# A new order of the seven products of a pair, and whole transposes with ScalarE copies in the late attention bursts

## The chip, the core and the metric

The kernel runs as one program on one core of a Trainium2 chip. The metric is the device time of one execution in microseconds (us); lower is better. A core has a matrix engine (TensorE, "PE" in the profile; its weight loads are listed apart as "PEld"), a vector engine (VectorE, "DVE"), a scalar engine (ScalarE, "ACT"), a general engine (GpSimd, "POOL") and an engine that here only issues DMAs (SyncE, "SP"). Each engine runs its own instructions in the order in which the program holds them, and waits on semaphores for the others.

## The reference

Chunked attention, and on its result a feed-forward layer with softplus, all in float32:

```python
# q, k, v: (8, 8, 576, 64); chunks of 64 positions
scores = scale * np.matmul(q_c, k_c.transpose(0, 1, 2, 4, 3))
scores = scores - np.max(scores, axis=-1, keepdims=True)
attn = np.exp(scores)
attn = attn / (np.sum(attn, axis=-1, keepdims=True) + 1e-09)
out = np.matmul(attn, v_c)
# x = out as (4608, 512); w_in (512, 2048), w_out (2048, 512)
h = x @ w_in
g = np.maximum(h, 0.0) + np.log1p(np.exp(-np.abs(h)))
return g @ w_out
```

## The kernel before

**The work.** A float32 operand is split into a high and a low part, and a product becomes three matmuls (high by high, low by high, high by low). The 4608 rows of x are nine blocks of 512; `w_in` is cut into 16 column chunks of 128, and `w_out` into 16 row chunks. For the first three blocks each chunk is one group of 12 matmuls for `x @ w_in` (L644) and one group of 12 for `g @ w_out` (L1004, called G2).

**The pairs.** The six later blocks are taken two at a time, in three *supers* (0, 1 and 2). In a super, two blocks and two chunks of `w_in` make a 2 by 2 product of block matrices, which is done with seven products of half the size in place of eight. This is a *pair*; a super has eight (named 0_0 to 0_7, and so on). `product(w, k)` issues product k: six matmuls (L788). The seven go into four PSUM banks, `BANK = (0, 1, 2, 3, 1, 2, 0)`: products 4, 5 and 6 add to the banks 1, 2 and 0. The banks lie in two PSUM tiles of two banks each, taken from a pool `pa` of two: one tile has the banks 0 and 3, the other the banks 1 and 2.

Around them stand small operations on 128 by 512 elements:
- the holds s0, s1 and s2 (`hold`, ScalarE, L794) copy bank 0, 1 and 2 to SBUF before the bank is added to;
- the mixes (`mix`, L807): d and c22 on GpSimd, e, f, f2 and c11 on VectorE. e reads bank 3, f reads bank 1, f2 bank 2, c11 bank 0; d needs s1 and s2, c22 needs d and e;
- four softplus operations (`soft`, ScalarE, L818, in super 2 L816): 10 reads bank 1, 01 reads bank 2, 11 reads the result of c22, and 00 that of c11.

The weights of a pair come from DRAM by two DMAs that GpSimd issues (`ring_load`, L745): part 0 (1024 KB) for products 0 to 3, part 1 (768 KB) for products 4 to 6. Each part has one buffer in supers 0 and 1, which is free when product 3, or product 6, is done.

**The order on PE.** In supers 0 and 1 a pair is the seven products, then two G2 groups of the pair before it; the second half of each super is G2 groups alone, for which the softplus results come back from DRAM (`spill_load`) and are split by ScalarE (`sp_hi`, L656) and VectorE (`sp_lo`, L660). In super 2 the second layer is done by seven products too (`sum_product`, L940, groups R): a pair is followed by two groups of six matmuls for the pair before, R1 and R0, and after the eight pairs come the groups R2 to R6.

**The attention bursts.** The attention of the later tiles of 128 rows runs beside this. A *burst* is two steps on PE (L608 and L520), each of which takes one `pa` tile: attention times values for two tiles, and the scores of the next two. Bursts stand after the pairs 2, 5 and 7 of supers 0 and 1 and once in each of their second halves. Between two bursts VectorE subtracts the maximum (L565, L570), ScalarE takes the exponential (L583), VectorE normalizes (L588 to L595) and turns the result. `blk_e4` does that with four transposes of 32 by 256 elements in each of two steps, Tf and Te (L544), so eight for a tile.

**What sets the order.** Nothing is ordered by hand but the list `seq` of PE's groups. `Plan` holds all tasks with an engine, a cost, what they need and an urgency, and plays them through ahead of time: a free engine takes the ready task with the lowest `urg`, and a task of `urg` 0 or more is held back when an urgent one is known to be ready within 0.5 us. The program's instructions are written in the order of the start times of this play. `take` names the pool slots that a task needs, and who frees them. The waits themselves aren't in the plan: the framework adds them from what each instruction reads and writes.

Of the kernel before, what the change touches and what calls it, by code (L numbers as in the profile page):

```python
# [160 lines left out]
def chunked_attention_softplus_ffn(  # L161
# [9 lines left out]
    nc = tc.nc  # L171
# [213 lines left out]
    def po_tile(n):  # L385
        return ps_o.tile([P, DM], F32, name=f"po{n}")
# [150 lines left out]
    def blk_e4(i, a):  # L537
# [126 lines left out]
    )  # L664
    X_SUMS = {0: ALU.add, 2: ALU.subtract, 3: ALU.add, 4: ALU.subtract, 6: ALU.add}
    BANK = (0, 1, 2, 3, 1, 2, 0)
    NX = 4
    PLACE = (1, 2, 0, 3, 6, 4, 5)

# [105 lines left out]
        eng.tensor_tensor(lo, x_of_product(n, k), hi.bitcast(F32), op=ALU.subtract)  # L775

    def product(w, k):
        if "bank" not in w:
            if w["in_po"]:
                w["bank"] = [po_tile(n) for n in range(4)]  # L780
            else:
                a, b = pa_tile(), pa_tile()
                w["bank"] = [a[:, 0], b[:, 0], b[:, 1], a[:, 1]]
        wts = w_image(w, k).rearrange("p (q k f) -> p q k f", q=2, k=2)
        hi, lo = (t.rearrange("p (k c) -> p k c", k=2) for t in x_image(k))
        for c in range(2):
            for n, (q, x) in enumerate(((0, hi), (1, hi), (0, lo))):
                nc.tensor.matmul(  # L788
                    w["bank"][BANK[k]], wts[:, q, c, :], x[:, c, :], start=k < NX and c + n == 0, stop=c == 1 and n == 2,
                    skip_group_check=True,  # L790
                )
# [3 lines left out]

    def mix(w, what):
        s1, s2, s3, f = (tmp_of(n) for n in range(4))
        x, y, z, v = w["bank"]
        out, a, b, op = {
            "d": (s2, s3, s2, ALU.subtract),  # L800
            "e": (s1, s1, v, ALU.add),
            "c22": (s1, s1, s2, ALU.add),
            "f": (f, y, s2, ALU.add),
            "f2": (f, f, z, ALU.subtract),
            "c11": (f, f, x, ALU.add),
        }[what]
        (nc.gpsimd if what in MIX_POOL else nc.vector).tensor_tensor(out, a, b, op=op)  # L807
# [92 lines left out]
    GI = 4  # L900

    def slot_of(k, j):
        return k + 4 * (j == FC // 2 - 2) if k < 2 else (FC // 2 * k + j + 2) % GI

    def g_image(k, j):
        if ("gi", k, j) not in live:
# [335 lines left out]
    for n in range(len(SUPERS)):  # L1242
        mine = pairs[n * FC // 2 : (n + 1) * FC // 2]
        for w in mine:
            seq += [f"P{k}_{w['name']}" for k in range(7)]
            seq += [f"G2_{v_['name']}" for v_ in behind[:1]]
            add_burst(n, 0, w["j"])
            seq += [f"G2_{v_['name']}" for v_ in behind[1:]]
            if n in BOTH and R_LAG <= w["j"] < FC // 2 - 1:
                seq += [f"R{k}_{w['j'] - R_LAG}" for k in (1, 0)]  # L1250
            behind = [] if n in BOTH else w["first"][::-1]
        if n in BOTH:
            NJ = FC // 2
# [40 lines left out]
    for key, (pv, ps) in bursts.items():  # L1294
# [40 lines left out]
        for n in range(2):  # L1335
# [11 lines left out]
            plan.add(f"norm{i}", "POOL" if pool else "DVE", 1.05 if pool else 0.65, partial(att_norm, i),  # L1347
                     [f"den{i}"], urg=d)
            gone = [f"V{FIRST_BLK - 1}"] if ps == F else [f"B{at}_{n}"]
            if i in SWAP_DVE:  # L1350
                plan.add(f"Tf{i}", "DVE", 1.76, partial(blk_e4, i, 0), [f"norm{i}"] + gone, urg=d)
                plan.add(f"Te{i}", "DVE", 1.76, partial(blk_e4, i, 1), [f"Tf{i}"], urg=d)
                swapped[i] = f"Te{i}"
            else:
                plan.add(f"Te{i}", "DVE", 0.65, partial(blk_e, i), [f"norm{i}"], urg=d)
                plan.add(f"swap{i}", "ACT" if i in SWAP_ACT else "SP", 4.8, partial(blk_swap, i), [f"Te{i}"] + gone, urg=d - SW_URG, kb=190, parts=8)
                swapped[i] = f"swap{i}"
# [55 lines left out]
    for at, w in enumerate(pairs):  # L1413
# [12 lines left out]
                     after=[f"ring{part}_{pairs[at - 1]['name']}"] if at else [])  # L1426
        for k in range(7):
            needs = [f"ring{k // NX}_{name}", f"xH{n}_{k}", f"xL{n}_{k}"]
            needs += [before[f"P{k}_{name}"]] + {4: [f"s1_{name}", f"s2_{name}"], 6: [f"s0_{name}", f"e_{name}"]}.get(k, [])
            take = []  # L1430
            if k == 0:
                rel = [[f"c11_{name}"], [f"soft10_{name}"], [f"soft01_{name}", f"f2_{name}"], [f"e_{name}"]]
                take = [("pa", rel[0] + rel[3]), ("pa", rel[1] + rel[2])]
                if w["in_po"]:
                    take = [(f"po{b}", rel[b]) for b in range(4)]
            plan.add(f"P{k}_{name}", "PE", PM, partial(product, w, k), needs, urg=1e6, take=take)
        for q in range(3):
            past = [f"soft00_{pairs[at - 1]['name']}", f"soft11_{pairs[at - 1]['name']}"] if at and not q else []
            plan.add(f"s{q}_{name}", "ACT", 0.59, partial(hold, w, q), [f"P{max(q, 2 * (q > 0))}_{name}"] + past, urg=-3 if n in BOTH else -2)
        for what, needs in (  # L1440
            ("d", ["s1", "s2"]), ("e", ["s0", "P3"]), ("c22", ["e", "d"]), ("f", ["d", "P5"]), ("f2", ["f", "P5"]),
            ("c11", ["f2", "P6"]),
        ):
            pool = what in MIX_POOL
            plan.add(f"{what}_{name}", "POOL" if pool else "DVE", 1.3 if pool else 0.69, partial(mix, w, what),
                     [f"{t}_{name}" for t in needs], urg=-2)
        a, b = (v_["name"] for v_ in w["first"])
        for i, jj, what in ((1, 0, "P5"), (0, 1, "P5"), (1, 1, "c22"), (0, 0, "c11")):
            kept = [f"lo{v_['name']}" for v_ in w["second"]] if j == FC // 2 - 1 else [f"us{name}"]
# [225 lines left out]
```

## Time and profile before

| what | value |
|---|---|
| runs shown | 829.07, 829.46 and 833.96 us, median 829.46 |
| the profiled execution | 831.35 us, its span in the profile 829.6 us |
| PE | busy 809.9 us, 98% of the span |
| PEld, DVE, ACT, POOL | 80%, 70%, 49%, 49% |
| granted TensorE clock | 0.995 |

The span goes from the first instruction to the last; the 1.75 us between it and the execution's own time lie outside of it. A busy time counts an engine from the start to the end of its instructions. Matmuls overlap: one of 512 columns is listed with 0.39 us, while the next starts 0.227 us after it. So the cost of a wait on PE is best read from the starts. A group of 12 that waits for nothing takes 2.72 us from its start to the start of the next, a product of six 1.36 us.

In the rows below, a row of the timeline has the start, the time, the engine, the source line, the operation and its operands, the count of instructions merged, and in brackets the idle time of the engine just before, with what ended it. A row of the waits has the engine and line that waited, what it waited for, the sum in us, how many times, and the longest. A row of the chain has start, time, engine and line, and the count.

### The profile page before, as it was taken

How to read it: one execution, taken by the hardware profiler on the slowest of the kernel's cores; microseconds unless marked ns; L12 is line 12 of the kernel's file. 1: busy time of each engine (PE TensorE's matmuls, PEld its weight loads, DVE VectorE, ACT ScalarE, POOL GpSimd, SP SyncE). 2: the span in 40 equal slices, each digit the busy share in tenths (PEclk: the TensorE clock that was granted, in tenths of full speed). 3: DMA queues.
4: the chain of work that ended last, by engine and by line, in shares of the span. 5: the costliest groups of instructions: out<-in, count | busy, mean ns of one | idle time of the engine just before them, and what ended most of it. 6: DMA issues, size and time to landing. Idle time of an engine off the chain costs nothing.

```text
span 829.6 us, 15582 instructions
## 1 busy us (share of the span) xinstructions
PE 809.9 (98%) x5675; PEld 661.9 (80%) x5675; DVE 581.2 (70%) x938; ACT 403.2 (49%) x664; POOL 404.3 (49%) x467
## 2 busy tenths in 40 slices
PE   8799999999999999999999999999999999999997
PEld 7687878888887888787888878888887788788786
DVE  4898997086478777657477878483789954575984
ACT  3767765345344574253434444443553644454551
POOL 1557559879975822221234212122177629982213
PEclk9899999999999999999999999999999999999999
DMA  9976758644674454777739527857647664566463
GB/s 218 239 187 190 207 164 244 188 112 127 149 198 113 111 146 158 219 187 213 197 127 257 158 64 242 227 153 213 203 130 258 209 228 167 202 234 231 150 206 68
DMA packets 202877, 151.27 MB, mean 182 GB/s; under 512 B 161136, under 2 KB 176752, under 8 KB 198576
## 3 DMA queue, kind: packets, MB, share of 16 engines
q1 hardware_dynamic: 189424, 99.66, 43.9%
q0 software_dynamic: 11232, 50.34, 18.9%
q8 instruction: 45, 0.74, 0.4%
q10 hardware_dynamic: 2144, 0.26, 0.2%
q14 instruction: 32, 0.26, 0.1%
HBM read 106.95 MB, written 41.94 MB: 179 GB/s over the span
## 4 chain that ended last, share of the span: by engine, by line
PE 77%; DVE 8%; DMA 4%; ACT 4%; POOL 3%; issue 3%; SPq 1%; DVEq 0%; POOLq 0%; ACTq 0%
PE po L1004 28%; PE pa L788 22%; PE pa L644 13%; PE po L940 9%; DVE g_lo L660 2%; PE pa L608 2%; DMA xb<-scratch 2%; PE pa L520 1%; DVE wib L807 1%; DMA images<-wib 1%; DVE ends L306 1%; POOL raw L875 1%; DVE eT L544 1%; DMA raw<-in_moe_w_in_dram 1%; POOL raw L865 1%
## 5 line engine op out<-in xcount | busy, mean ns | idle before, releaser
L807 POOL TENSOR_TENSOR wib<-wib 128x512 f32<-128x512 f32 x48 | 63.0, 1312 | 207.9 <-ACT wib L794 198.5
L1004 PE MATMUL po<-late,g_hi 128*128 128x512 f32 x420 | 128.8, 392 | 0.1
L544 DVE STREAM_TRANSPOSE eT<-qe 32x256 f32<-32x256 f32 x216 | 93.9, 435 | 3.0
L788 PE MATMUL pa<-wi_hi,xb 128*128 128x512 f32 x304 | 93.9, 390 | 0.4 <-DMA xb<-scratch 0.4
L1004 PEld LDWEIGHTS po<-late,g_hi 128*128 128x128 f32 x420 | 78.2, 188 | 16.9 <-DVE raw L1011 0.4
L788 PE MATMUL pa<-wib,xb 128*128 128x512 f32 x360 | 87.2, 395 | 0.7 <-DVE wib L775 0.7
L1004 PE MATMUL po<-wo_hi,g_lo 128*128 128x512 f32 x224 | 84.4, 393 | 0.8 <-DVE g_lo L660 0.7
L1004 PE MATMUL po<-wo_hi,g_hi 128*128 128x512 f32 x224 | 85.1, 396 | 0.0
L1004 PE MATMUL po<-wo_lo,g_hi 128*128 128x512 f32 x224 | 84.2, 392 | 0.0
L1004 PE MATMUL po<-late,g_lo 128*128 128x512 f32 x224 | 83.5, 390 | 0.3 <-DVE g_lo L660 0.3
L788 PEld LDWEIGHTS pa<-wib,xb 128*128 128x128 f32 x360 | 65.9, 188 | 18.7 <-ACT wib L794 4.5
L807 DVE TENSOR_TENSOR wib<-wib,pa 128x512 f32<-128x512 f32 x72 | 49.3, 685 | 42.4 <-PE pa L788 26.8
L660 DVE TENSOR_TENSOR g_lo<-ends,g_hi 128x512 fp32r<-128x512 f32 x64 | 53.3, 832 | 29.3 <-ACT g_hi L656 29.0
L652 ACT ACTIVATE u<-pa 128x512 f32<-128x512 f32 (+1 forms) x50 | 29.0, 579 | 92.2 <-PE pa L644 87.8
L794 ACT COPY wib<-pa 128x512 f32<-128x512 f32 x72 | 39.8, 587 | 56.9 <-PE pa L788 56.9
L656 ACT CAST g_hi<-ends 128x512 fp32r<-128x512 f32 x64 | 39.5, 617 | 57.6 <-PE po L1004 53.2
L788 PEld LDWEIGHTS pa<-wi_hi,xb 128*128 128x128 f32 x304 | 56.8, 188 | 13.1 <-issue 1.4
L788 PE MATMUL pa<-wi_lo,xb 128*128 128x512 f32 x152 | 59.2, 389 | 0.0
L660 DVE TENSOR_TENSOR g_lo<-u,g_hi 128x512 fp32r<-128x512 f32 (+1 forms) x32 | 31.1, 971 | 31.8 <-ACT g_hi L656 24.9
L1004 PEld LDWEIGHTS po<-wo_hi,g_lo 128*128 128x128 f32 x224 | 42.3, 189 | 10.9 <-DVE g_lo L660 2.1
L1004 PEld LDWEIGHTS po<-late,g_lo 128*128 128x128 f32 x224 | 42.0, 188 | 9.6 <-DVE g_lo L660 0.9
L1004 PEld LDWEIGHTS po<-wo_lo,g_hi 128*128 128x128 f32 x224 | 42.3, 189 | 8.7
(288 smaller groups left out, 1777.7 us busy)
## 6 DMA issues: line engine op xcount, KB each, us to landing
xb<-scratch POOLq DMA_DIRECT2D x19, 1024.0 KB, 6.0
xb<-scratch POOLq DMA_DIRECT2D x20, 768.0 KB, 7.1
raw<-in_moe_w_in_dram SPq DMA_DIRECT2D x16, 512.0 KB, 5.3
raw<-in_moe_w_out_dram SPq DMA_DIRECT2D x16, 512.0 KB, 5.0
scratch<-ends SPq DMA_DIRECT2D x16, 512.0 KB, 3.0
out_dram<-raw SPq DMA_DIRECT2D x28, 256.0 KB, 3.4
spill<-ends SPq DMA_DIRECT2D x14, 512.0 KB, 5.1
ends<-spill SPq DMA_DIRECT2D x14, 512.0 KB, 4.1
```

The costliest lines, as they stand in the source:

```text
L306: nc.vector.tensor_tensor(low, low, live.pop(("top", u)), op=ALU.add)
L544: nc.vector.transpose(live["eT", i][d : d + BL, tb], e[s : s + BL, kb])
L608: nc.tensor.matmul(pa[o, a, col : col + C], vt[r, 4 * j + 2 * h2 + c2, :], eT[r, :, 4 * c2 + 2 * j + h2, :], start=True, stop=True,)
L644: nc.tensor.matmul(ph, wt[:, c, :], x[:, ts_, c, :], start=(n == 0), stop=(n == 3 * KC - 1))
L652: nc.scalar.activation(w["u"], w["ph"], AF.Softplus)
L656: nc.scalar.copy(w["hi"], w["u"])
L660: (nc.gpsimd if pool else nc.vector).tensor_tensor(w["lo"], w["u"], w["hi"].bitcast(F32), op=ALU.subtract)
L788: nc.tensor.matmul(w["bank"][BANK[k]], wts[:, q, c, :], x[:, c, :], start=k < NX and c + n == 0, stop=c == 1 and n == 2, skip_group_check= ...
L794: nc.scalar.copy(tmp_of(n), w["bank"][n])
L807: (nc.gpsimd if what in MIX_POOL else nc.vector).tensor_tensor(out, a, b, op=op)
L940: nc.tensor.matmul(live["acc", ACC[k]][ct][:, cols], (w[:, q] if k > 1 else w[q])[:, ct * P : (ct + 1) * P], g[:, cols], start=k < 3 and j ...
L1004: nc.tensor.matmul(pos[w["m"]][t], terms[n][0][:, j * P : (j + 1) * P], terms[n][1], start=(w["first"] and n == 0), stop=n == 2 and (w["la ...
```

## The change

- In every pair the products run in the order 1, 2, 0, 3, 4, 5, 6. The two PSUM tiles are no longer taken together at the first product: that of the banks 1 and 2 is taken at product 1, that of the banks 0 and 3 at product 0.
- In a pair without a burst, one of the two G2 groups (in super 2: R1) moves from behind product 6 to between products 3 and 4. In a pair with a burst it stays between product 6 and the burst.
- The plan's needs follow: each hold needs its own product alone; product 4 needs s1, product 5 needs s2; a hold waits for the last readers of its own place of the pair before.
- For the tiles from 22 on (14 tiles) `blk_e2` transposes the whole 128 by 512 tile twice in place of the eight quarters, once into each of two buffers, and `blk_cross` has ScalarE copy four blocks of 32 by 256 from the one into the other. The burst's second step then needs these copies.

```diff
+    def blk_e2(i, a):
+        e = live["e", i].rearrange("p a j (u k) -> p u (a j) k", u=2)
+        if a == 0:
+            nc.vector.transpose(live["eA", i], e)
+            return
+        live["eT", i] = blk_et(i)
+        nc.vector.transpose(live["eT", i], e)
+        live.pop(("e", i))
+
+    def blk_cross(i):
+        ea, eT = live.pop(("eA", i)), live["eT", i]
+        for a in range(2):
+            for kb in range(2):
+                d, s = (2 * a + kb) * BL, (2 * a + 1 - kb) * BL
+                nc.scalar.copy(eT[d : d + BL, 1 - kb], ea[s : s + BL, kb])
...
+    ORDER = (1, 2, 0, 3, 4, 5, 6)
...
     def product(w, k):
-        if "bank" not in w:
-            if w["in_po"]:
-                w["bank"] = [po_tile(n) for n in range(4)]
-            else:
-                a, b = pa_tile(), pa_tile()
-                w["bank"] = [a[:, 0], b[:, 0], b[:, 1], a[:, 1]]
+        if k in (ORDER[0], ORDER[2]):
+            t = pa_tile()
+            w.setdefault("bank", {}).update({1: t[:, 0], 2: t[:, 1]} if k == 1 else {0: t[:, 0], 3: t[:, 1]})
...
     def slot_of(k, j):
-        return k + 4 * (j == FC // 2 - 2) if k < 2 else (FC // 2 * k + j + 2) % GI
+        return k + 4 * (j == FC // 2 - 1) if k < 2 else (FC // 2 * k + j + 2) % GI
...
+    CROSS = tuple(range(22, NPT))
...
-            seq += [f"P{k}_{w['name']}" for k in range(7)]
-            seq += [f"G2_{v_['name']}" for v_ in behind[:1]]
-            add_burst(n, 0, w["j"])
-            seq += [f"G2_{v_['name']}" for v_ in behind[1:]]
-            if n in BOTH and R_LAG <= w["j"] < FC // 2 - 1:
-                seq += [f"R{k}_{w['j'] - R_LAG}" for k in (1, 0)]
+            j = w["j"]
+            mid, end = (behind[:1], behind[1:]) if len(behind) > 1 else ([], behind)
+            mid, end = ([f"G2_{v_['name']}" for v_ in vs] for vs in (mid, end))
+            if n in BOTH and j >= R_LAG:
+                mid, end = [f"R1_{j - R_LAG}"], [f"R0_{j - R_LAG}"]
+                if j == FC // 2 - 1:
+                    mid, end = [], mid + end
+            burst_here = (n, 0, j) in bursts
+            seq += [f"P{k}_{w['name']}" for k in ORDER[:4]] + ([] if burst_here else mid)
+            seq += [f"P{k}_{w['name']}" for k in ORDER[4:]] + (mid if burst_here else [])
+            add_burst(n, 0, j)
+            seq += end
...
+            if i in CROSS:
+                plan.add(f"Tf{i}", "DVE", 0.69, partial(blk_e2, i, 0), [f"norm{i}"] + gone, urg=d)
+                plan.add(f"Te{i}", "DVE", 0.69, partial(blk_e2, i, 1), [f"Tf{i}"], urg=d)
+                plan.add(f"Tc{i}", "ACT", 1.6, partial(blk_cross, i), [f"Te{i}"], urg=d)
+                swapped[i] = f"Tc{i}"
...
-            needs += [before[f"P{k}_{name}"]] + {4: [f"s1_{name}", f"s2_{name}"], 6: [f"s0_{name}", f"e_{name}"]}.get(k, [])
+            needs += [before[f"P{k}_{name}"]] + {4: [f"s1_{name}"], 5: [f"s2_{name}"], 6: [f"s0_{name}", f"e_{name}"]}.get(k, [])
             take = []
-            if k == 0:
-                rel = [[f"c11_{name}"], [f"soft10_{name}"], [f"soft01_{name}", f"f2_{name}"], [f"e_{name}"]]
-                take = [("pa", rel[0] + rel[3]), ("pa", rel[1] + rel[2])]
+            if k == ORDER[0]:
+                take = [("pa", [f"soft10_{name}", f"soft01_{name}", f"f2_{name}"])]
+            elif k == ORDER[2]:
+                take = [("pa", [f"c11_{name}", f"e_{name}"])]
...
-            plan.add(f"s{q}_{name}", "ACT", 0.59, partial(hold, w, q), [f"P{max(q, 2 * (q > 0))}_{name}"] + past, urg=-3 if n in BOTH else -2)
+            plan.add(f"s{q}_{name}", "ACT", 0.59, partial(hold, w, q), [f"P{q}_{name}"] + past, urg=-3 if n in BOTH else -2)
```

More of the change, by code (lines that the diff above doesn't have):

```diff
@@ L797, in mix @@
         s1, s2, s3, f = (tmp_of(n) for n in range(4))
-        x, y, z, v = w["bank"]
+        x, y, z, v = (w["bank"][n] for n in range(4))
         out, a, b, op = {
@@ L1253, in chunked_attention_softplus_ffn @@
             NJ = FC // 2
-            seq += [f"R{k}_{j}" for j in range(NJ - R_LAG - 1, NJ) for k in (1, 0)]
+            seq += [f"R{k}_{j}" for j in range(NJ - R_LAG, NJ) for k in (1, 0)]
             seq += [f"R{k}_{j}" for k in range(2, 6) for j in range(NJ if k < 5 else NJ - SPREAD)]
@@ L1349, in chunked_attention_softplus_ffn @@
             gone = [f"V{FIRST_BLK - 1}"] if ps == F else [f"B{at}_{n}"]
-            if i in SWAP_DVE:
+            if i in CROSS:
[3 more added lines that the diff above has]
+                swapped[i] = f"Tc{i}"
+            elif i in SWAP_DVE:
                 plan.add(f"Tf{i}", "DVE", 1.76, partial(blk_e4, i, 0), [f"norm{i}"] + gone, urg=d)
@@ L1428, in chunked_attention_softplus_ffn @@
             needs = [f"ring{k // NX}_{name}", f"xH{n}_{k}", f"xL{n}_{k}"]
-            needs += [before[f"P{k}_{name}"]] + {4: [f"s1_{name}", f"s2_{name}"], 6: [f"s0_{name}", f"e_{name}"]}.get(k, [])
+            needs += [before[f"P{k}_{name}"]] + {4: [f"s1_{name}"], 5: [f"s2_{name}"], 6: [f"s0_{name}", f"e_{name}"]}.get(k, [])
             take = []
-            if k == 0:
-                rel = [[f"c11_{name}"], [f"soft10_{name}"], [f"soft01_{name}", f"f2_{name}"], [f"e_{name}"]]
-                take = [("pa", rel[0] + rel[3]), ("pa", rel[1] + rel[2])]
-                if w["in_po"]:
-                    take = [(f"po{b}", rel[b]) for b in range(4)]
+            if k == ORDER[0]:
+                take = [("pa", [f"soft10_{name}", f"soft01_{name}", f"f2_{name}"])]
+            elif k == ORDER[2]:
+                take = [("pa", [f"c11_{name}", f"e_{name}"])]
             plan.add(f"P{k}_{name}", "PE", PM, partial(product, w, k), needs, urg=1e6, take=take)
         for q in range(3):
-            past = [f"soft00_{pairs[at - 1]['name']}", f"soft11_{pairs[at - 1]['name']}"] if at and not q else []
-            plan.add(f"s{q}_{name}", "ACT", 0.59, partial(hold, w, q), [f"P{max(q, 2 * (q > 0))}_{name}"] + past, urg=-3 if n in BOTH else -2)
+            past = [f"{t}_{pairs[at - 1]['name']}" for t in (("soft11",), ("c22", "f"), ("d",))[q]] if at else []
+            plan.add(f"s{q}_{name}", "ACT", 0.59, partial(hold, w, q), [f"P{q}_{name}"] + past, urg=-3 if n in BOTH else -2)
         for what, needs in (
@@ L1444, in chunked_attention_softplus_ffn @@
             pool = what in MIX_POOL
+            past = [f"soft00_{pairs[at - 1]['name']}"] if at and what == "f" else []
             plan.add(f"{what}_{name}", "POOL" if pool else "DVE", 1.3 if pool else 0.69, partial(mix, w, what),
-                     [f"{t}_{name}" for t in needs], urg=-2)
+                     [f"{t}_{name}" for t in needs] + past, urg=-2)
         a, b = (v_["name"] for v_ in w["first"])
```

## The prediction

> **What bounds the kernel now.** I read the page's head first, then who PE and its weight loads wait for from 317 us on, where the pairs begin.
>
> ```profile
> span 829.6 us, 15582 instructions
> PE 809.9 (98%) x5675; PEld 661.9 (80%) x5675; DVE 581.2 (70%) x938; ACT 403.2 (49%) x664; POOL 404.3 (49%) x467
> ...
> 317.00:487.00 170.00, 169.61 (x1215) 138.56 (x1214) 116.72 (x206) 74.48 (x119) 45.10 (x59) 1.00 0.67 189
> ...
> PE pa L788 <- DMA xb<-scratch: 0.4, 2, 0.2
> ...
> PEld pa L788 <- ACT wib L794: 6.2, 24, 0.9
> PEld po L1004 <- DVE g_lo L660: 3.0, 5, 1.1
> ...
> PEld pa L788 <- DVE wib L775: 1.1, 1, 1.1
> ```
>
> PE is the bound: its matmuls fill 98% of the span, and from 317 to 487 us all but 0.39 of 170 us. The change adds and removes no matmul, and nothing before the first pair moves. So it can only gain what PE waits, and lose what it makes PE wait. The head hides the small waits; the weight loads show them. One number stands out: 24 waits for a hold (L794), and there are 24 pairs.
>
> ```profile
> 729.67 9.62 PE pa L788 x42
> 739.29 2.72 PE po L940 x12
> ...
> 366.61 1.07 ACT L794 COPY wib<-pa 128x512 f32<-128x512 f32 x2 [0.69 <-PE pa L788]
> 367.74 1.23 PEld L788 LDWEIGHTS pa<-wib,xb 128*128 128x128 f32 x6 [0.23 <-ACT wib L794]
> ...
> 371.95 0.39 PE L1004 MATMUL po<-wo_hi,g_hi 128*128 128x512 f32 x1
> ...
> 710.22 1.66 PE L788 MATMUL pa<-wib,xa 128*128 128x512 f32 x6 [0.52 <-ACT wib L794]
> ```
>
> Twelve matmuls in 2.72 us make 0.227 each, so a pair's 42 should take 9.52; the chain gives 9.62. The missing 0.10 lies at product 4: s1 and s2, both after product 2, end at 367.68, and the weights of product 4 come at 367.74, 0.06 behind. Product 4 writes bank 1 and s2 reads bank 2, so the wait is for the whole two-bank tile.
>
> **The change part by part.** First what PE gets back. Listed idle understates a loss: a matmul is listed with 0.39 but its successor starts after 0.227, so 0.16 is to be added, and about 0.10 for the restart (the same 0.10 as above).
>
> *Holds.* With the order 1, 2, 0, 3 both holds are done two products or more before product 4. 23 ordinary waits at 0.10 are 2.3 us; the long one, in pair 2_3 (0.52 + 0.16 + 0.10), is 0.8. If holds are late on ScalarE, products 0 and 3 (2.72 us), and in most pairs a group besides, cover them.
>
> *Ring loads and the first pair of super 1.*
>
> ```profile
> 382.83 1.30 POOL L807 TENSOR_TENSOR wib<-wib 128x512 f32<-128x512 f32 x1 [9.88 <-ACT wib L794]
> 385.01 1.30 POOL L807 TENSOR_TENSOR wib<-wib 128x512 f32<-128x512 f32 x1 [0.89 <-DVE wib L807]
> 386.25 0.57 POOL L745 DMA_DIRECT2D xb<-scratch  x1
> ...
> xb<-scratch POOLq DMA_DIRECT2D x20, 768.0 KB, 7.1
> ...
> 392.83 0.70 PE L788 MATMUL pa<-wi_hi,xb 128*128 128x512 f32 x2 [0.21 <-DMA xb<-scratch]
> ...
> 497.96 1.19 PE L788 MATMUL pa<-wib,xb 128*128 128x512 f32 x4 [0.69 <-DVE wib L775]
> ```
>
> Counted back from the wait at 392.83 (two groups, 5.44, and products 4 to 6, 4.18), product 3 is done at about 383. But part 0 of the next weights is issued at 386.25, behind d and c22 on GpSimd's queue. Now d starts when products 1 and 2 are held, so it is over before product 3 ends, and the load can go some 3 us sooner; PE's way from product 3 to the next pair stays the same length. Two waits of 0.2 + 0.16 + 0.10 go: 0.9 us. Part 1 has less room before a burst pair (one group less, 8.2 us from product 6 to product 4), but lands in 7.1 even now, while part 0 is under way beside it; I price it at 0. The wait at 497.96 is product 6 for its x image; a G2 group now stands between, so 0.69 + 0.16 + 0.10 = 0.95 goes.
>
> *The transposes.*
>
> ```profile
> L544 DVE STREAM_TRANSPOSE eT<-qe 32x256 f32<-32x256 f32 x216 | 93.9, 435 | 3.0
> L532 DVE STREAM_TRANSPOSE ka<-qe x5: 698/705/711, 70.8 to 283.6; 128x512 f32<-128x512 f32 x5
> L656 ACT CAST g_hi<-ends 128x512 fp32r<-128x512 f32 x64 | 39.5, 617 | 57.6 <-PE po L1004 53.2
> L660 DVE TENSOR_TENSOR g_lo<-ends,g_hi 128x512 fp32r<-128x512 f32 x64 | 53.3, 832 | 29.3 <-ACT g_hi L656 29.0
> ...
> 653.37 1.01 ACT L879 CAST wib<-wib 128x256 fp32r<-128x256 f32 x3
> ...
> 630.57 1.80 DVE L544 STREAM_TRANSPOSE eT<-qe 32x256 f32<-32x256 f32 x4
> 633.53 1.23 DVE L660 TENSOR_TENSOR g_lo<-ends,g_hi 128x512 fp32r<-128x512 f32 x1
> 634.81 0.50 PE L1004 MATMUL po<-wo_hi,g_lo 128*128 128x512 f32 x1 [0.68 <-DVE g_lo L660]
> ```
>
> Eight quarters at 0.435 are 3.48 us a tile; two whole ones (nearest row: the same operation at L532, 0.705) are 1.41. VectorE gets back 2.07 on each of 14 tiles, 29 us. ScalarE gets four copies a tile; no row has 32 by 256, the nearest is 128 by 256, three in 1.01, so 1.3 us for four, at most 1.6, some 20 in all on an engine that is 49% busy. On PE this is worth only what stood behind transposes: the five waits for g_lo. Their 3.0 us of idle weight loads, less 0.13 each by the measure above (0.23 of idle cost 0.10), are 2.35 on PE. The longest is at 634.81, behind a row of four quarters and the next tile's work; I take three of the five, 1.4 us, between bounds of 0 and 2.35. Against it: a set of copies can stand before a g_hi on ScalarE. A group lasts 2.72, and hi (0.62) and lo (0.83) with their hand-overs need some 1.6, so 1.6 us of copies costs at most 0.5, in the four tiles whose copies fall in second halves: 2.0 at worst, taken as 0.
>
> One rule of the Trainium skill speaks against this 1.4: "SBUF — State Buffer", section "Who interferes with whom", has a VectorE instruction with two SBUF inputs shut out while GpSimd reads SBUF. That would leave g_lo slow (1.23 here) whatever the transposes take, and the sum at 0 to 0.7 for this term.
>
> Together: 2.3 + 0.8 + 0.9 + 0.95 + 1.4 = 6.35 us.
>
> *What the new order makes PE wait for.* Product 1 now opens a pair, and takes the PSUM tile of banks 1 and 2, which the pair before gives back after softplus 10 and 01, f and f2. Before, product 0 opened with the other tile.
>
> ```profile
> 370.84 1.28 ACT L818 ACT_TABLE_LOAD   x1 [3.15 <-PE pa L788]
> 372.83 0.69 DVE L807 TENSOR_TENSOR wib<-pa,wib 128x512 f32<-128x512 f32 x1 [2.42 <-ACT ends L818]
> 374.28 0.60 ACT L818 ACTIVATE ends<-pa 128x512 f32<-128x512 f32 x1 [1.55 <-DVE wib L807]
> ...
> 726.33 0.69 DVE L807 TENSOR_TENSOR wib<-pa,wib 128x512 f32<-128x512 f32 x1 [2.77 <-ACT wo_hi L816]
> 727.06 0.60 ACT L816 ACTIVATE wo_lo<-pa 128x512 f32<-128x512 f32 x1 [0.83 <-DVE wib L807]
> 727.69 1.48 DVE L807 TENSOR_TENSOR wib<-wib,pa 128x512 f32<-128x512 f32 x2 [0.67 <-ACT wo_lo L816]
> ...
> 726.79 0.62 PE L940 MATMUL po<-g_hi,wo_hi 128*128 128x512 f32 x2
> ...
> ACT L818 <- PE pa L788: 14.8, 5, 3.1
> ACT L816 <- PE pa L788: 3.1, 1, 3.1
> ```
>
> The readers of this tile go one after another, across engines and banks: f starts when softplus 10 ends, softplus 01 (bank 2) when f (bank 1) ends, f2 when softplus 01 ends. In super 2 product 6 starts at 726.79 - 1.36 = 725.43, and f2, the first of the last two, ends at 727.69 + 0.69 = 728.38: 2.95 later. Product 1 will be due 2.72 after product 6 (itself and one R group). Wait: 0.23 + 0.06 + 0.10 = 0.39, after the six pairs 2_1 to 2_6: 2.3 us. In supers 0 and 1 a G2 group follows in place of R0, and product 1 is due 4.08 later: nothing, except where ScalarE must reload the softplus table. There (product 6 at 371.95 - 1.36 = 370.59) the last reader ends at 374.88, 4.29 later: 0.21 + 0.06 + 0.10 = 0.37. The six table loads, five and one, make 2.2 us. No earlier wait stands here, so nothing hides this; behind product 1 all of PE is queued.
>
> Sum: 829.6 - 6.35 + 2.3 + 2.2 = 827.75 us of span, 1.85 less. The profiled execution (831.35, span and 1.75 around it) would be 829.5; it lay 1.9 over the median of the runs shown, so I take the difference to the median: 829.46 - 1.85 = **827.6**.
>
> **The rivals.**
>
> *Each bank is freed by its own readers.* Then product 1 waits for f alone, 1.6 us after product 6 began, and the 4.5 us of new waits vanish: 829.46 - 6.35 = 823.1. For it: softplus 10 and f end long before. Against it: product 4 waiting for s2, and softplus 01 for f, of the other bank. In the Trainium skill, "PSUM — Partial Sum Buffer", section "PSUM bank collisions raise a hardware error", asks to guard PSUM by bank and quadrant, which would give this time; the rows above show wider waits.
>
> *Slower: VectorE is late for f in super 2.* The chain behind product 5 has no slack left, so each operation that stands before f on VectorE is paid by PE. Once it is so already:
>
> ```profile
> 763.23 0.69 DVE L897 TENSOR_TENSOR late<-late,late 128x512 f32<-128x512 f32 x1
> 763.85 0.68 DVE L807 TENSOR_TENSOR wib<-pa,wib 128x512 f32<-128x512 f32 x1
> ```
>
> f waits there for a subtraction of super 2 that it does not need. At about 0.5 in six pairs the time is 827.6 + 3 = 830.6. It decides from 1.85 us, 0.3 a pair. Against it: in the pair at 726.33 f starts right behind softplus 10.
>
> *The holds stop PE.* If s1 stood before product 2 in the program, product 2 would wait for it (same tile): 0.20 + 0.55 + 0.06 + 0.10, about 0.9 in 24 pairs, some 850. Against it: the plan starts product 2 the moment product 1 ends and s1 0.15 later.
>
> **How the numbers follow.** My sum: 0.60. Banks apart: 0.20. VectorE late, or other new waits of that size: 0.15. Holds stop PE: 0.03; 0.02 for gains larger than all I count. The forecast alone, with 1.4 between 0 and 2.35 and the copies up to 2.0, goes from 826.6 to 831; with the first rival the range is 822.5 to 830.8. One per cent (8.3 us) is about what a measurement can tell from no change: faster by that 0.02, within it 0.94, slower 0.04.
>
> **What would show it.** In the changed profile the 42 products no longer lose 0.10 at product 4, and the waits for L794 and for the ring loads are gone. Right: PE waits at product 1 for L807 or L818, 0.2 to 0.3 us, about twelve times. Wrong: no such wait (the first rival), or waits of 0.7 in super 2, or product 2 waiting for L794. Whole transposes should take 0.7, four copies 1.3. The prediction fails too if g_hi comes late behind copies.

## The result and the profile after

The changed kernel takes 835.50 us (median of 13 runs, 833.51 to 838.82) against 830.13 us (13 runs beside it, 828.27 to 833.96): a ratio of 1.0070, 95% interval 1.0056 to 1.0083. It is 5.4 us slower; 827.6 had been forecast, with a range up to 830.8. (One execution of a later run, regroup, took 1755.02 us, with the matmuls of a product listed at 0.67 us each throughout, and its profile is left aside.)

The head of the page:

```profile
span 835.2 us, 15496 instructions
PE 808.9 (97%) x5675; PEld 662.9 (79%) x5675; DVE 552.1 (66%) x854; ACT 426.2 (51%) x720; POOL 406.2 (49%) x467
```

VectorE lost 29 us of work and ScalarE gained 23, about as forecast, and PE has the same 5675 matmuls. The span is still 5.6 us longer, so PE waits more. For whom, the waits of PE's weight loads tell, from 317 us on (who waited, for whom, sum, times, longest):

```profile
PEld pa L802 <- ACT ends L832: 6.5, 5, 1.5
PEld pa L802 <- DVE wib L821: 4.2, 6, 1.5
PEld po L1018 <- DVE g_lo L676: 2.7, 2, 2.5
...
PEld pa L802 <- ACT wib L808: 1.3, 2, 0.7
PEld pa L802 <- ACT ends L830: 0.5, 1, 0.5
```

(L802 is a product, L808 a hold, L821 a mix, L830 and L832 the softplus, L1018 a G2 group: 14 lines further down than before.) The 24 waits for a hold are now two. In their place stand 5 + 6 + 1 = 12 waits for a softplus or a mix. Twelve were forecast, but at 0.2 to 0.3 us each on PE. Here the weight loads' longest is 1.5, and on PE itself five of the twelve are 1.23, as the starts show.

Read by the starts (what two successive matmuls are apart beyond 0.227 us, added up from the first product to the end), PE lost 9.4 us before and loses 14.7 now. From the start of the first product to the last instruction of an engine it takes 513.6 us against 508.4; in front of that the changed program is the same, and differs by 0.4 (in other runs by up to 3). Where the loss sits, in us, restarts counted in:

| place | before | after | forecast for after |
|---|---|---|---|
| product 1, or the first of a pair | 0.95 (two ring loads) | 9.39 (twelve tile waits) | 4.5 |
| product 4 | 2.58 | 1.01 | 0 |
| product 6 | 0.97 | 0 | 0 |
| G2 groups, for g_lo and behind bursts | 3.47 | 3.31 | about 2.1 |
| first steps of the bursts, and R groups | 1.40 | 0.97 | 1.4 |

The twelve: 0.26 behind pairs 1_0 and 2_0, 0.28 behind 2_1 to 2_4 and 2_6, and 1.23 behind 0_3, 0_6, 1_3, 1_6 and 2_5, each with 0.11 for the restart. One of the long ones, behind 0_3, in the timelines of PE, ScalarE and VectorE:

```profile
370.36 4.24 PE L802 MATMUL pa<-wib,xb 128*128 128x512 f32 x18
378.39 0.73 PE L802 MATMUL pa<-wi_hi,xb 128*128 128x512 f32 x2 [1.07 <-ACT ends L832]
```

```profile
373.28 1.65 ACT L562 COPY eT<-ka 32x256 f32<-32x256 f32 x4 [4.86 <-DVE eT L554]
375.09 1.28 ACT L832 ACT_TABLE_LOAD   x1 [0.16 <-DVE wib L821]
376.39 0.60 ACT L832 ACTIVATE ends<-pa 128x512 f32<-128x512 f32 x1
377.74 0.60 ACT L832 ACTIVATE ends<-pa 128x512 f32<-128x512 f32 x1 [0.76 <-DVE wib L821]
```

```profile
374.37 0.65 DVE L821 TENSOR_TENSOR wib<-pa,wib 128x512 f32<-128x512 f32 x1
377.02 1.48 DVE L821 TENSOR_TENSOR wib<-wib,pa 128x512 f32<-128x512 f32 x2 [2.00 <-ACT ends L832]
```

Product 6 starts at 370.36 + 2.72 = 373.08. Just then the second transpose of a tile is done, and its four copies stand in front of the table load and softplus 10 in ScalarE's queue. They and f, which now comes first, hold the table load up until 375.09. Then comes the known chain: table load, softplus 10, f2, softplus 01 (bank 2), which ends at 378.34, 5.26 after product 6 began. (Behind a table load f2 comes ahead of softplus 01, in the kernel before too; the order softplus 01, then f2 is that of super 2.) Product 1 was due at 373.08 + 4.08 = 377.16 and starts at 378.39, 1.23 late. In the profile before, the same chain ended 4.29 after. ScalarE's list of waits tells it a second time: four table loads now wait for a mix, where before all five waited for PE.

```profile
ACT L832 <- DVE wib L821: 0.6, 4, 0.2
```

Gains that were forecast are there too: a pair without a wait takes 9.52 in the chain (9.62 before), and the waits for ring loads and for the x image of 1_0 are gone.

```profile
521.04 9.52 PE pa L802 x42
```

### The profile page after: what moved, and what is told of

It reads as the page before. It is cut to its first block, busy times and chain, and to the rows that moved or that the text cites. A ratio compares the mean times of both kernels' runs of the same rounds, so it can differ in the third digit from the quotient of the medians.

```text
span 835.2 us, 15496 instructions
## 1 busy us (share of the span) xinstructions
PE 808.9 (97%) x5675; PEld 662.9 (79%) x5675; DVE 552.1 (66%) x854; ACT 426.2 (51%) x720; POOL 406.2 (49%) x467
## 4 chain that ended last, share of the span: by engine, by line
PE 76%; DVE 9%; ACT 4%; DMA 4%; issue 3%; SPq 2%; POOL 2%; DVEq 0%; ACTq 0%; POOLq 0%
PE po L1018 30%; PE pa L802 22%; PE pa L660 13%; PE po L954 8%; DVE wib L821 2%; SPq L359 2%; PE pa L624 2%; PE pa L520 1%; DVE g_lo L676 1%; DMA raw<-in_moe_w_in_dram 1%; DVE qe L611 1%; DMA q<-in_q_dram 1%; DVE qe L507 1%; ACT ends L832 1%; DMA raw<-in_moe_w_out_dram 1%
## 5 line engine op out<-in xcount | busy, mean ns | idle before, releaser
L821 POOL TENSOR_TENSOR wib<-wib 128x512 f32<-128x512 f32 x48 | 65.6, 1366 | 192.8 <-ACT wib L808 174.7
L1018 PE MATMUL po<-late,g_hi 128*128 128x512 f32 x420 | 128.7, 391 | 0.0
L802 PE MATMUL pa<-wi_hi,xb 128*128 128x512 f32 x304 | 94.6, 393 | 5.7 <-ACT ends L832 4.3
L1018 PEld LDWEIGHTS po<-late,g_hi 128*128 128x128 f32 x420 | 78.3, 188 | 16.5
L1018 PE MATMUL po<-wo_hi,g_lo 128*128 128x512 f32 x224 | 84.2, 392 | 2.1 <-DVE g_lo L676 2.1
L802 PE MATMUL pa<-wib,xb 128*128 128x512 f32 x360 | 85.1, 390 | 0.5 <-ACT wib L808 0.5
L1018 PE MATMUL po<-wo_hi,g_hi 128*128 128x512 f32 x224 | 85.1, 396 | 0.0
L1018 PE MATMUL po<-wo_lo,g_hi 128*128 128x512 f32 x224 | 84.1, 392 | 0.0
L1018 PE MATMUL po<-late,g_lo 128*128 128x512 f32 x224 | 83.4, 390 | 0.0
L821 DVE TENSOR_TENSOR wib<-wib,pa 128x512 f32<-128x512 f32 x72 | 49.5, 687 | 46.5 <-ACT wib L808 23.9
L802 PEld LDWEIGHTS pa<-wib,xb 128*128 128x128 f32 x360 | 67.4, 188 | 15.3 <-ACT wib L808 1.3
L802 PEld LDWEIGHTS pa<-wi_hi,xb 128*128 128x128 f32 x304 | 56.4, 188 | 20.4 <-ACT ends L832 6.5
L676 DVE TENSOR_TENSOR g_lo<-ends,g_hi 128x512 fp32r<-128x512 f32 x64 | 48.2, 759 | 33.2 <-ACT g_hi L672 33.1
L808 ACT COPY wib<-pa 128x512 f32<-128x512 f32 x72 | 40.6, 588 | 53.6 <-PE pa L802 53.5
L802 PE MATMUL pa<-wi_lo,xb 128*128 128x512 f32 x152 | 59.2, 389 | 0.0
L762 POOL DMA_DIRECT2D xb<-scratch x39 | 22.1, 567 | 65.4 <-PE pa L802 50.2
L821 DVE TENSOR_TENSOR wib<-pa,wib 128x512 f32<-128x512 f32 x24 | 16.4, 683 | 54.9 <-ACT ends L832 28.3
L1018 PEld LDWEIGHTS po<-wo_hi,g_lo 128*128 128x128 f32 x224 | 42.3, 189 | 11.5 <-DVE g_lo L676 2.5
L1018 PEld LDWEIGHTS po<-wo_lo,g_hi 128*128 128x128 f32 x224 | 42.3, 189 | 8.7
```

Of the source, the lines that this page charges most:

```text
L676: (nc.gpsimd if pool else nc.vector).tensor_tensor(w["lo"], w["u"], w["hi"].bitcast(F32), op=ALU.subtract)
L762: on("ring").dma_start(t[:, : cols.stop - cols.start], src[:, cols])
L802: nc.tensor.matmul(w["bank"][BANK[k]], wts[:, q, c, :], x[:, c, :], start=k < NX and c + n == 0, stop=c == 1 and n == 2, skip_group_check= ...
L808: nc.scalar.copy(tmp_of(n), w["bank"][n])
L1018: nc.tensor.matmul(pos[w["m"]][t], terms[n][0][:, j * P : (j + 1) * P], terms[n][1], start=(w["first"] and n == 0), stop=n == 2 and (w["la ...
```

## The experiments

All times beside runs of the kernel before on the same chip. "Length" is from the first product to the end; "lost" is the excess of the starts, as above. The length of before is 508.4. Length and loss come from one execution of each kernel: the two of groups_mixed differ by 0.4 in length.

| kernel | median us | ratio to before, 95% | length | lost | at product 1 | at 4 | at 6 |
|---|---|---|---|---|---|---|---|
| after | 835.50 | 1.0070 (1.0056 to 1.0083) | 513.6 | 14.7 | 9.39 | 1.01 | 0 |
| order_only | 829.94 | 1.0009 (0.9995 to 1.0024) | 508.4 | 9.4 | 5.86 | 0 | 0 |
| cross_only | 828.41 | 0.9983 (0.9963 to 1.0002) | 506.6 | 7.6 | 0.11 | 2.26 | 0.97 |
| copies_late | 830.69 | 1.0006 (0.9988 to 1.0024) | 508.0 | 9.2 | 5.66 | 0 | 0 |
| cross_pool | 833.04 | 1.0034 (1.0017 to 1.0051) | 510.7 | 11.7 | 6.25 | 0 | 0 |
| vhi_after | 834.41 | 1.0042 (1.0022 to 1.0061) | 511.7 | 13.0 | 8.64 | 1.01 | 0 |
| regroup | 829.70 | 0.9987 (0.9964 to 1.0011) | - | - | - | - | - |
| regroup_again | 828.16 | 0.9966 (0.9948 to 0.9984) | 506.2 | 7.8 | 0 | 4.11 | 0 |
| regroup_late | 828.24 | 0.9987 (0.9970 to 1.0004) | 506.3 | 7.7 | 0 | 4.05 | 0 |
| groups_behind | 826.65 | 0.9957 (0.9938 to 0.9977) | 504.7 | 6.3 | 0 | 0 | 2.95 |
| groups_behind_no_cross | 827.77 | 0.9969 (0.9944 to 0.9994) | 505.1 | 6.6 | 0 | 0 | 2.89 |
| groups_mixed | 824.50 | 0.9924 (0.9902 to 0.9946) | 502.9 | 4.3 | 0.36 | 0 | 0.49 |
| groups_mixed_2 | 824.89 | 0.9927 (0.9901 to 0.9954) | 502.5 | 4.2 | 0.37 | 0 | 0.49 |

### Each half of the change alone

order_only is the changed kernel with the quarter transposes of before:

```diff
-    CROSS = tuple(range(22, NPT))
+    CROSS = ()
```

> The new order of the products with the old eight quarter transposes on VectorE, no copies on ScalarE. Theory A (the copies stand in front of softplus 10 on ScalarE): product 1 waits only 0.3 to 0.4 us behind pairs 0_3, 0_6, 1_3 and 1_6 as it does behind 1_0 and 2_0, and product 4 of 0_7 and 1_7 waits no more; the time falls by about 4.9 us against the changed kernel, to 0 to 1.5 us over the kernel before. Rival B (VectorE reaches f late, whatever ScalarE does): four quarters hold VectorE longer than whole transposes, so the waits of 1.2 us stay or grow, and the time stays 5 to 6 us over the kernel before.

cross_only is the kernel before with the new transposes and copies alone:

```diff
+    CROSS = tuple(range(22, NPT))
...
-            if i in SWAP_DVE:
+            if i in CROSS:
+                (Tf, Te and Tc as in the change)
+            elif i in SWAP_DVE:
```

> The old order of the products, with two whole transposes and four copies for the tiles from 22 on. Theory A: the copies delay softplus 10 here too, but the first product of the next pair comes 6.8 us after the start of product 6 in place of 4.1, so nothing waits for it; product 4 may wait longer for its holds in pairs 0_7 and 1_7. Time: within 1.5 us of the kernel before. Rival C (the copies cost PE time by themselves, through late holds or late g_hi): 3 us or more over the kernel before.

The order alone costs nothing on balance (length 508.4 as before), the transposes alone gain 1.8 us of length (0.95 at the G2 groups and 0.84 at the ring loads; the ratio's interval still reaches 1.0002), and together they lose 5.2. So the two halves hurt each other. But cross_only does not show the copies under cover, as its expectation had it: they stand behind the softplus there. Behind 0_3 they start at 373.27, 5.7 after product 6 began, and the last reader of the tile ends 4.28 after it, as in the kernel before. The same pair in order_only, ScalarE and VectorE:

```profile
371.26 1.28 ACT L832 ACT_TABLE_LOAD   x1 [4.89 <-PE pa L802]
372.56 0.60 ACT L832 ACTIVATE ends<-pa 128x512 f32<-128x512 f32 x1
374.71 0.60 ACT L832 ACTIVATE ends<-pa 128x512 f32<-128x512 f32 x1 [1.55 <-DVE wib L821]
```

```profile
369.31 3.56 DVE L544 STREAM_TRANSPOSE eT<-qe 32x256 f32<-32x256 f32 x8
373.26 0.69 DVE L821 TENSOR_TENSOR wib<-pa,wib 128x512 f32<-128x512 f32 x1 [0.39 <-ACT ends L832]
```

Without copies the table load waits for PE alone, and softplus 01 ends at 375.31. Product 6 began at 371.02, so that is 4.29 later, the forecast's own number; all six waits behind table loads are 0.26. The eight quarter transposes stand on VectorE in the meantime and delay nothing: f comes 0.10 behind softplus 10.

### The copies, moved in time and to another engine

copies_late holds the four copies until softplus 00 of the next pair has been issued; cross_pool gives them to GpSimd.

```diff
+                hold_back = [f"soft00_{key[0]}_{key[2] + 1}"] if not key[1] and key[2] < FC // 2 - 1 else []
-                plan.add(f"Tc{i}", "ACT", 1.6, partial(blk_cross, i), [f"Te{i}"], urg=d)
+                plan.add(f"Tc{i}", "ACT", 1.6, partial(blk_cross, i), [f"Te{i}"], urg=d, after=hold_back)
```

> The changed kernel, with the copies of a burst's tiles held back until softplus 00 of the next pair has been issued. Theory A: as order_only, the waits of 1.2 us behind 0_3, 0_6, 1_3 and 1_6 fall to 0.3 to 0.4; 4 to 5 us faster than the changed kernel, 0 to 1.5 us over the kernel before. Rival B (VectorE late for f): no faster than the changed kernel by more than 1 us.

```diff
-                nc.scalar.copy(eT[d : d + BL, 1 - kb], ea[s : s + BL, kb])
+                nc.gpsimd.tensor_copy(eT[d : d + BL, 1 - kb], ea[s : s + BL, kb])
...
-                plan.add(f"Tc{i}", "ACT", 1.6, partial(blk_cross, i), [f"Te{i}"], urg=d)
+                plan.add(f"Tc{i}", "POOL", 2.0, partial(blk_cross, i), [f"Te{i}"], urg=d)
```

> The changed kernel with the four copies of a tile on GpSimd in place of ScalarE. Theory A (the copies cost because they stand in front of softplus 10 and the holds on ScalarE): the waits of 1.23 at product 1 behind 0_3, 0_6, 1_3 and 1_6 fall to 0.26 and the two at product 4 vanish; 2_5 keeps its 1.2. GpSimd has no such copy yet; its additions of 128 by 256 take 0.73, so four copies some 2 to 3 us; what of it stands in front of d, c22 or a ring load may cost up to 0.5 a pair. 508 to 510 from the first pair to the end, time 830 to 831. Theory B (the two whole transposes on VectorE, ahead of f, make the 1.23): the four waits stay at 1 or more, 833 or more.

In both, the four waits of 1.23 fall to 0.26 and the two at product 4 vanish, while the two whole transposes stay ahead of f on VectorE. So it is the copies on ScalarE, at that place, and not the transposes. The place of f goes with that of the copies: in both runs f stands behind softplus 10 again (behind 0_3 in copies_late it starts 0.10 after softplus 10 ends). In the changed kernel the plan has f in front, and f ends at 375.02, 0.09 after the copies; which of the two alone would have held the table load was not run. ScalarE in copies_late:

```profile
374.24 1.28 ACT L832 ACT_TABLE_LOAD   x1 [4.90 <-PE pa L802]
375.53 0.60 ACT L832 ACTIVATE ends<-pa 128x512 f32<-128x512 f32 x1
...
380.74 1.65 ACT L562 COPY eT<-ka 32x256 f32<-32x256 f32 x4
```

cross_pool is still slower than copies_late, and its length of 510.7 is above the 508 to 510 expected: its G2 groups lose 4.4 us (2.6 there), and one product 1 waits 0.7 more. Four copies on GpSimd take 4 x 0.43 us, less than expected:

```profile
L562 POOL COPY eT<-ka 32x256 f32<-32x256 f32 x56 | 24.2, 431 | 17.1 <-DVE eT L554 14.7
```

Which of GpSimd's work they delay there was not followed up.

### The fifth long wait, behind 2_5

No copies run in super 2. ScalarE at this place in the changed kernel:

```profile
744.37 0.41 ACT L893 CAST raw<-raw 128x256 fp32r<-128x256 f32 x1 [2.88 <-POOL raw L889]
744.68 0.60 ACT L830 ACTIVATE wo_hi<-pa 128x512 f32<-128x512 f32 x1
```

softplus 10 stands behind a cast of the image sums (L893) that waits for GpSimd. vhi_after puts this cast behind softplus 10:

```diff
-                plan.add(f"vh{j}_{i}", "ACT", 0.4, partial(v_hi, j, i), [f"vs{j}_{i}"], urg=d + 3)
+                plan.add(f"vh{j}_{i}", "ACT", 0.4, partial(v_hi, j, i), [f"vs{j}_{i}"], urg=d + 3,
+                         after=[f"soft10_{n}_5"] if (j, i) == (NJ - 1, 1) else [])
```

> The changed kernel, with one cast of the image sums (v_hi, L893) placed behind softplus 10 of pair 2_5 in the plan. Theory A (in 2_5 softplus 10 is late because ScalarE takes its instructions in order and a cast that waits for GpSimd stands in front of it): the wait of 1.23 at product 1 behind 2_5 falls to 0.28, the other eleven stay: 512.7 from the first pair to the end against 513.6, time 834.6. Theory B (VectorE's subtractions of super 2, L911, make f late): it stays at 1.2 and the time at 835.5.

```profile
742.66 0.60 ACT L830 ACTIVATE wo_hi<-pa 128x512 f32<-128x512 f32 x1 [2.23 <-PE pa L802]
```

softplus 10 now waits for PE alone, and the wait at product 1 behind 2_5 falls from 1.23 to 0.28 (that behind 2_4 rises by 0.16). The length falls by 1.9: 0.8 from here, and 1.2 because the wait for g_lo at 652 us was 1.00 in place of 2.24 in this execution. The program there is the same, so that part comes and goes between executions.

### The tile, paired otherwise

regroup lets banks 1 and 3 share the tile that product 1 takes, and banks 2 and 0 the one that product 2 takes; regroup_again is the same kernel, regroup_late adds the late copies of above.

```diff
-        if k in (ORDER[0], ORDER[2]):
+        if k in ORDER[:2]:
             t = pa_tile()
-            w.setdefault("bank", {}).update({1: t[:, 0], 2: t[:, 1]} if k == 1 else {0: t[:, 0], 3: t[:, 1]})
+            w.setdefault("bank", {}).update({1: t[:, 0], 3: t[:, 1]} if k == 1 else {2: t[:, 0], 0: t[:, 1]})
...
             if k == ORDER[0]:
-                take = [("pa", [f"soft10_{name}", f"soft01_{name}", f"f2_{name}"])]
-            elif k == ORDER[2]:
-                take = [("pa", [f"c11_{name}", f"e_{name}"])]
+                take = [("pa", [f"soft10_{name}", f"f_{name}", f"e_{name}"])]
+            elif k == ORDER[1]:
+                take = [("pa", [f"c11_{name}", f"soft01_{name}", f"f2_{name}"])]
```

> The changed kernel with other banks in one PSUM tile: 1 with 3, and 2 with 0 (before: 1 with 2, 0 with 3). Order, groups and copies stay. Theory T (an access to a two-bank tile waits for the other bank's accesses too): product 1 then needs only softplus 10, f and e of the pair before, so all twelve waits at product 1 go, some 9 us against the changed kernel, to 3 to 5 us under the kernel before. Rival U (the waits follow the bank, or softplus 10 and f themselves are late): product 1 waits as it does now and the time stays 4 to 6 us over the kernel before.

> The changed kernel with the banks paired otherwise: 1 and 3 share the tile that product 1 takes, 2 and 0 the one that product 2 takes; a second profile of the kernel of the run regroup. Theory A (PE waits for the whole tile, and for its last reader): product 1 now waits for softplus 10, f and e alone, which end 3.8 us after product 6 began at the latest (4.08 are there), so the twelve waits at product 1 go, 9.4 us of PE with their restarts; product 2 is due 5.4 after product 6 began and its last readers end 5.3 after it at worst; only behind pair 2_5 some 0.6 is left. The two waits of product 4 (0.8) and one for g_lo (1 to 2) stay. 335.2 to 504 of PE from the first pair to the end, against 513.6 in the changed kernel; time 825.5. Theory B (PE loses time at the head of a pair for another reason, such as the new order of the banks or the weights): the twelve losses stay, and the time is 829 or more.

> The banks paired as in regroup_again, and the four copies of a tile held until softplus 00 of the next pair has been issued. Theory A: no wait at product 1, and no product 4 waits for a hold behind copies: besides the 0.73 of the burst's own restarts only g_lo (about 1.2) and pair 2_6 (0.6) are left, 503 from the first pair to the end, time 825. If the copies alone were to blame (theory C) and not the tile, pairing the banks otherwise adds nothing to holding the copies back (830.7 measured in copies_late): 830.

(The 335.2 in the second of these is a slip; the length meant is 504.) All twelve waits at product 1 are gone in both, 9.4 us of PE: it was the tile's last reader that PE waited for. The two waits of product 4 behind copies, which were expected to stay in regroup_again, are gone as well. But the length is 2.2 and 3.3 above what was expected, and the medians are 0.8 to 2.4 us under the kernel before in place of 3 to 5, since a new wait appeared that no theory had: product 4 in three pairs of super 2 (four in regroup_late). In regroup_again, PE and VectorE:

```profile
681.86 4.39 PE L802 MATMUL pa<-wib,xa 128*128 128x512 f32 x18 [1.21 <-DVE wib L821]
```

```profile
679.11 1.37 DVE L938 TENSOR_TENSOR g_lo<-ends,g_hi 128x512 fp32r<-128x512 f32 x1 [2.03 <-ACT g_hi L934]
680.52 0.69 DVE L911 TENSOR_TENSOR ends<-ends 128x512 f32<-128x512 f32 x1
681.13 0.68 DVE L821 TENSOR_TENSOR wib<-wib,pa 128x512 f32<-128x512 f32 x1
```

Product 4 writes bank 1; the mix that ends at 681.81, 0.05 before it, is e, which reads bank 3. They now share a tile, so product 4 waits for e and for what stands ahead of e on VectorE.

### The groups put back behind product 6

groups_behind keeps the new order, the banks and the copies, but has both groups behind product 6 as before; groups_behind_no_cross does so with the quarter transposes.

```diff
             burst_here = (n, 0, j) in bursts
+            if not burst_here:
+                mid, end = [], mid + end
```

> The changed kernel, but both groups (G2, or R1 and R0) stay behind product 6 as in the kernel before, also in pairs without a burst; banks, order of products and copies as changed. Theory A: product 1 comes 6.8 us (in super 2 4.1) after product 6 began, later than the last reader of its tile (5.26, in super 2 2.95), so the twelve waits go, 9.4 us; in super 2 behind 2_5 some 0.1 to 0.3 is left. The first pair of super 1 waits for its x image again at product 6 (0.97). 504 from the first pair to the end, time 825 to 826. Theory B (the loss at product 1 comes with the order 1, 2, 0, 3 itself): the waits stay, 834.

> As groups_behind, with the eight quarter transposes of the kernel before in place of two whole transposes and four copies. Theory A: waits at product 1 and 4 gone here too, since neither depends on the copies once the groups stand behind product 6; what is left is g_lo (1.4 as in order_only), the x image in the first pair of super 1 (0.97) and perhaps the ring loads (0.5): 504 to 505 from the first pair to the end, time 826. If the transposes by themselves are worth more than the 1.8 us that cross_only showed, it lies 3 us or more above groups_behind.

With one more group in front of product 1 the twelve waits are gone, with copies and without, and both are faster than before. But the chain of 5.26 was not put under 6.8 us of cover, as the expectation had it: in this order the plan places the copies behind the softplus. Behind 0_3 they start at 375.23, 5.7 after product 6 began, and the last reader of the tile ends 4.28 after it; behind 0_6, 1_3 and 1_6 it is the same. Two things came back for want of a group between products 3 and 4: the x image of 1_0 (0.97, expected) and a wait for e in 0_1 (1.33, not expected: quarters of an early tile stand ahead of e). Another for e in 2_6 is 0.38. In groups_behind:

```profile
337.21 0.96 PE L802 MATMUL pa<-wib,xb 128*128 128x512 f32 x3 [1.17 <-DVE wib L821]
```

```profile
334.70 1.73 DVE L544 STREAM_TRANSPOSE eT<-qe 32x256 f32<-32x256 f32 x4
336.47 0.69 DVE L821 TENSOR_TENSOR wib<-wib,pa 128x512 f32<-128x512 f32 x1
```

groups_mixed leaves a group between the products in these two pairs alone.

```diff
+            if not burst_here and (n, j) not in ((0, 1), (1, 0)):
+                mid, end = [], mid + end
```

> As groups_behind, but in the two pairs 0_1 and 1_0 a group stands between products 3 and 4 as in the changed kernel: there it gives e, and the x image of product 6, time. Theory A: product 6 no longer waits for e in 0_1 (1.33 and 0.1 of restart in groups_behind) nor for its x image in 1_0 (0.91 and 0.1); product 1 behind 0_1 has 4.1 us and its last reader needs 3 without a table load, so no wait there; behind 1_0, which loads the table, it waits 0.26 and 0.11. Net gain on groups_behind 2.1: 502.6 from the first pair to the end, time 824.5. Theory B (a group between products is no help to e; VectorE just does the same work later): 0_1 still waits, 826 or more.

> The kernel of groups_mixed once more, for its time beside that of the kernel before: 824.5 to 825.5 if the 502.9 from the first pair to the end is right, 5.5 under before; a ratio of 0.993 to 0.994.

This is the fastest of the versions: 824.50 and 824.89 us in two sets of six runs, 0.75% under the kernel before, some 10.8 us under the changed one. Its page and its waits, in the second set:

```profile
span 823.0 us, 15515 instructions
PE 804.9 (98%) x5675; PEld 662.4 (80%) x5675; DVE 556.9 (68%) x854; ACT 425.1 (52%) x720; POOL 409.1 (50%) x467
```

```profile
PEld po L1018 <- DVE g_lo L676: 2.2, 5, 1.3
PEld pa L802 <- DVE wib L821: 0.6, 1, 0.6
PEld pa L802 <- ACT ends L832: 0.5, 1, 0.5
```

Of the twelve waits one is left, behind 1_0 (0.26), where the group still stands between.

## Why the prediction was wrong, step by step

**The failed step** is "the last reader ends at 374.88, 4.29 later: 0.21 + 0.06 + 0.10 = 0.37. The six table loads, five and one, make 2.2 us." The mechanism, the place and the count were right. The 4.29 was read in the profile before, where no copies stood on ScalarE, and was carried over as if the change left that row alone. In four of the six pairs it became 5.26, and the term became 4 x 1.34 + 2 x 0.37 = 6.1 in place of 2.2; order_only, without copies, has 4.28 to 4.29 in all six. The prediction had the copies' 1.3 us of ScalarE, and asked what they could stand in front of, but only of g_hi ("taken as 0"), not of softplus 10, which is on the one chain that it had itself found to be without slack. Two more terms fell by what stands first in ScalarE's queue:

- *Holds*: 3.1 forecast, 2.58 lost before by the starts (an ordinary one cost 0.08, not 0.10), 1.57 gained. In 0_7 and 1_7 the copies stand between the holds s1 and s2, and product 4 still waits 0.40 (and restarts). Here in 0_7, where the first hold ends at 430.53, the next at 432.81 and product 4 starts at 432.86:

```profile
430.54 1.65 ACT L562 COPY eT<-ka 32x256 f32<-32x256 f32 x4
432.22 1.08 ACT L808 COPY wib<-pa 128x512 f32<-128x512 f32 x2
```

- *The waits of super 2*: 0.39 each was right to the hundredth in five of six (0.28 and 0.11). Behind 2_5 it is 1.34, for the cast that vhi_after moved.

*Ring loads*: 0.9 forecast, 0.95 gained, but not shown to come from the new order: cross_only, in the old order, loses 0.11 at these places. In the changed kernel the load for 0_5 is issued at 385.64, still behind d, 1.5 after product 3 ends (3.3 before), so 1.7 sooner and not 3. *The first pair of super 1*: 0.95 and 0.97. The R groups gave 0.4 that were not counted.

*The transposes*: 1.4 forecast between 0 and 2.35, 0.2 found in this execution. VectorE's relief was as forecast, the quarters of 0.43 giving way to whole ones of 0.68:

```profile
L551 DVE STREAM_TRANSPOSE ka<-qe 128x512 f32<-128x512 f32 x14 | 9.3, 687 | 0.0
L554 DVE STREAM_TRANSPOSE eT<-qe 128x512 f32<-128x512 f32 x14 | 9.2, 675 | 0.0
...
L562 ACT COPY eT<-ka 32x256 f32<-32x256 f32 x56 | 22.6, 404 | 21.5 <-DVE eT L554 20.8
```

But the longest wait for g_lo stands behind other work of VectorE, the x sums (L780):

```profile
649.97 3.44 DVE L780 TENSOR_TENSOR wib<-xa 128x1024 f32<-128x1024 f32 x2
653.34 1.21 DVE L676 TENSOR_TENSOR g_lo<-ends,g_hi 128x512 fp32r<-128x512 f32 x1
```

The longest wait for g_lo is 2.24 here, was 0.84 before, and is 0.94 to 1.22 in the other kernels but cross_pool (1.65). The G2 groups lose 2.3 to 2.9 us in those, against 3.47 before, so the gain there is 0.2 to 1.1; cross_only, where nothing else is changed, gained 1.0. But order_only, which keeps the quarters, gained 0.9 there as well, so what the whole transposes are worth to PE is not shown. The prediction had a rule of the Trainium skill against this term ("SBUF — State Buffer", "Who interferes with whom": a VectorE instruction with two SBUF inputs is shut out while GpSimd reads). The g_lo of 1.21 at 653.34 agrees with it, as GpSimd was at work beside it; the larger part of the wait is the queue in front.

The sum in its own terms: 1.57 + 0.95 + 0.97 + 0.16 + 0.43 = 4.1 gained, 9.4 lost, 5.3 slower; the length grew by 5.2.

**The rivals.** "Each bank is freed by its own readers" is wrong: product 1 (bank 1) starts 0.05 behind softplus 01 (bank 2) at 378.34, and when the banks are paired otherwise, product 4 (bank 1) waits for e (bank 3). The Trainium skill, "PSUM — Partial Sum Buffer", section "PSUM bank collisions raise a hardware error", asks for a guard by bank and quadrant; the waits of this kernel are wider than that, by tile. "VectorE is late for f in super 2" had the sign right, and even the place in one pair, but the engine wrong: it is ScalarE, and softplus 10 is late, not f. Its size would have been 0.95 of the 7.1 that the forecast was off. (The upper end of the range, 830.8, is a little below the 831 that the prediction's own bounds give.) "The holds stop PE" did not happen: product 2 never waits for L808.

**What would show it.** The twelve waits were there; "0.2 to 0.3 us" held for seven. "Waits of 0.7 in super 2" had been named as what proves the sum wrong, but not longer waits in supers 0 and 1. Four copies were to take 1.3; they take 1.65.

## What to carry to other kernels

When a change shortens the time between the last reader of a buffer and its next writer, the slack of that chain has to be worked out with everything the same change puts on the readers' engines: an engine that is idle half of the time still makes the chain late by what is left of the work that stands first in its queue (here 0.97 for copies of 1.65). Two halves that are each harmless can hurt together, so each is worth running alone. And a filler between dependent steps is worth placing step by step: of 24 pairs the group between the products paid in two and only cost in ten others; in 2_6 it cost 0.39 at product 1 and saved 0.49 at product 6.

## What the runs showed of the hardware

- A copy of 32 partitions by 256 takes ScalarE 0.404 us, as long as a cast of 128 by 256 (0.41), and four in a row take 1.65, one after the other, while two casts of 128 partitions overlap (0.71 for two). The timeline of ScalarE in the changed kernel:

```profile
702.11 0.71 ACT L893 CAST raw<-raw 128x256 fp32r<-128x256 f32 x2
```

  The quarter transposes on VectorE do not overlap either (eight of 0.434 in 3.56). The Trainium skill, "VectorE: DVE Perf Modes", section "Two Vector instructions with no wait between them", has, as a model, an instruction held whose input or output starts at another group of 32 partitions than that of the one before. VectorE's rows agree (two whole transposes, which all start at the same one, overlap: 1.29 for two of 0.69); that ScalarE's copies, which change the group each time, are held for the same reason was not tried.
- Moving the copies from ScalarE to GpSimd hardly changes their price (0.404 and 0.431 each), only whom they stand in front of.
- After a wait PE loses a further 0.11 us at its second matmul: in all twelve waits at product 1 and the two at product 4 of the changed kernel, and at product 6 in groups_behind. In the kernel before it is 0.08 after the two waits for ring loads.
